# Transposes in 64 by 64 blocks, scores by v in one step, and a new order with other holds and buffers

## The chip, the cores and the metric

The kernel runs on one core of a Trainium2 chip. The metric is the device time of one execution in microseconds; lower is better. About 1% (2.1 us) is what a measurement of this kernel can tell from no change.

## What is computed

A gated linear recurrence per batch and head gives x, and x goes through a two-matrix layer with a rational activation. Batch 4, 8 heads, 768 steps, head size 48; 3072 tokens of width 384; hidden width 2048.

```
f = 1 / (1 + exp(-f_logit))
for t in range(768):
    state = f[:, :, t, :, None] * state + outer(k[:, :, t], v[:, :, t])
    y[:, :, t] = q[:, :, t] @ state
x = y, heads side by side, (3072, 384)
h = x @ w_in                                   # (3072, 2048)
P = a0 + a1*h + a2*h**2 + a3*h**3
Q = 1 + |b0|*|h| + |b1|*h**2
out = (P / (Q + 1e-6)) @ w_out                 # (3072, 384) float32
```

## The kernel before

The work is cut into 12 units: three stretches of 256 steps for each of 4 batches. Unit n belongs to batch n % 4. A unit has two halves (j = 0, 1) of 128 steps; a partition holds two neighbouring steps (i = 0, 1), so 64 partitions stand for one half.

Each unit goes through the same steps. In the order of the data:

- `ld` loads f, k, q (queue of SyncE) and v (GpSimd's queue). `ef`, `ls` (ScalarE) make log-forget-gates, `cs` (TensorE) their running sums, `A` (ScalarE) the exponentials of them.
- `xa` multiplies q or k by these into `qk`, a half of the heads or all at a time, on VectorE or, with the letter p, on GpSimd. `vm` copies a piece of v into another layout, on either.
- `T` (TensorE) transposes `qk` into PSUM, `Te` copies it to SBUF (mostly ScalarE).
- `sc` (TensorE) makes the scores of two head pairs, `mk` (VectorE) multiplies them by the mask out of PSUM into `scm`. `yb` (TensorE) adds scores by v into y, `yi` adds q by the incoming state. `ic`, `si` (TensorE) and `st` (VectorE) make the next state. `ye` copies y out as x.
- `h` (TensorE) makes 4 of 16 blocks of the hidden layer in one PSUM slot, `hy` (ScalarE) copies them to SBUF. `p1`, `p2`, `pm` (VectorE) and `sq` (VectorE) or `sa` (ScalarE) build the numerator, `ab` and the sum `zv` (VectorE) or `zd` (an adding transfer issued by GpSimd) the denominator. `rq` (ScalarE) takes its reciprocal, `tv` (VectorE) or `ta` (an adding transfer) completes the numerator, `gm` (VectorE) multiplies. `o` (TensorE) makes the output, `oe` copies it, `so` stores it.

In the profile lines these are: `T` is L347, `Te` L357 and L358, `sc` L370, `mk` L378, `yb` and `yi` L391, `ic` L436, `si` L446, `st` L461, `xa` L333, `vm` L385, `h` L477, `hy` L489, `sq` L493, `sa` L498, `ab` L502, `zv` L507, `zd` L511, `rq` L516, `p1` L526, `p2` L531, `pm` L536, `ta` L540, `tv` L544, `gm` L548, `o` L557, `oe` L567, w_out loads L221, v loads L209.

What stands in which order on each engine is written out by hand in the table `ORDER`: steps with unit, range and PSUM slot (`@`). Each engine works through its own steps strictly in that order and waits only for data and buffers. Besides, a step can be marked (`!m3`) and another held behind the mark (`^m3`): the held one begins only when the marked instruction is done. Buffers of a unit come from rings; unit n uses buffer n modulo the ring's size:

```
for key, n in (("hy", 3), ("h2", 2), ("z", 2), ("g", 3), ("qi", 2)):
    rings(key, n, [KF, NT], BF16)
```

Of the kernel before, what the change touches and what calls it, by code (L numbers as in the profile page):

```python
# [8 lines left out]
F32 = mybir.dt.float32  # L9
# [10 lines left out]
cu 1; cz 1; ld 0 f 2 4; ld 0 v; ab_ b s; cz 3; cz 0; ld 0 f 0 2; ci; ld 0 q 2 4; ld 1 f; cu 0; ld 0 k 0 2  # L20
ef 0 2 4; ls 0 2 4; cm; ld 0 k 2 4; cz 2; fa; cs 0 2 4 @0; ef 0 0 2; ls 0 0 2; ld 0 q 0 2; cs 0 0 2 @1; ld 1 k
A 0 1 0 2; A 0 1 2 4; A 0 0 2 4; A 0 0 0 2; fr; ld 2 f; ef 1; xa 0 1 2 4; ls 1; xa 0 0 2 4; vm 0 v; cs 1 @2
xa 0 0 0 2; ld 1 q; xa 0 1 0 2 !m0; ld 1 v ^m0; ld 3 f; ic 0 @3; wi 2 8 16; A 1 1; wi 3 8 16; A 1 0
T 0 0 2 @0; st 0 0; ld 2 q; ab_ a s; wi 1 8 16; xa 1 1 2 4; T 0 2 4 @1; wi 0 8 16; Te 0 0 2 s; sc 0 0 @2
xa 1 0 0 2; Te 0 2 4 s; xa 1 0 2 4; ef 2; si 0 1; sc 0 1 @0; xa 1 1 0 2; st 0 1; T 1 @1; mk 0 0; ld 2 k
mk 0 1 !m5; yb 0 0 2 @3; yi 0 1; Te 1; ef 3; yb 0 2 4; ic 1 @2; ls 2; st 1 0 !m1; sc 1 1 @0; ld 2 v ^m1
ye 0 s; cs 2 @1; mk 1 1 !m3; ls 3; sc 1 0 @3; wi 0 0 8; A 2 0; si 1 1; ld 5 f; cs 3 @0; wi 3 0 8; st 1 1
A 2 1; vm 1 v !m4; wi 2 0 8; mk 1 0; xa 2 0 0 2 p ^m0; A 3 0; h 0 8 12 @2; wi 1 0 8; xa 2 0 2 4; h 0 12 16 @1
hy 0 8 12; cz 4; fb; ld 4 f; yb 1 0 2 @3; hy 0 12 16; yb 1 2 4; xa 2 1; yi 1 1; ye 1 s; p1 0 8 16; T 2 @2
A 3 1; ab 0 8 16; h 1 12 16 @1; Te 2 s; sq 0 8 16; h 1 8 12 @3; p2 0 8 16; hy 1 12 16; pm 0 8 16 !m2; ld 3 q  # L30
ic 2 @0; hy 1 8 12; vm 2 ^m2; sc 2 1 @2; st 2 0; sc 2 0 @1; mk 2 1 !m7; ld 3 k; si 2 1; ef 5; h 0 0 4 @3
st 2 1; ls 5; ld 6 f; ab 1 8 16; h 0 4 8 @2; ef 4; tv 0 8 16; hy 0 0 4; ld 4 k; xa 3 0 2 4 p ^m3; h 1 4 8 @0
mk 2 0; ls 4; ld 4 q; ld 3 v ^m3; hy 0 4 8; h 1 0 4 @3; xa 3 1; ld 4 v; hy 1 4 8; xa 3 0 0 2; yb 2 0 2 @1
ld 7 f; zv 0 8 16; hy 1 0 4; T 3 @2; p1 0 0 8; ef 6; yi 2 1; yb 2 2 4; sq 1 0 8; Te 3 s; cs 4 @0; ld 8 f
ye 2 s; ab 1 0 8; sc 3 0 @3; cs 5 @2; A 4 0; ab 0 0 8 !m11; xa 4 0 2 4 p ^m2; mk 3 0; A 4 1; ic 3 @1
sa 1 8 16; h 2 8 12 @0; st 3 0; ld 5 k; sq 0 0 8; si 3 1; h 2 12 16 @3; hy 2 8 12; pm 0 0 8; zd 0 0 8; ld 5 q
xa 4 1 2 4 p ^m5; ls 6; sc 3 1 @0; st 3 1 !m6; A 5 1; ld 6 k; vm 3 ^m4; mk 3 1; h 2 4 8 @1; ld 5 v; hy 2 12 16
xa 4 1 0 2; ef 7; yi 3 1 @0; xa 4 0 0 2; yb 3 0 2; wo 12 16; p1 1 8 16; hy 2 4 8; T 4 @3; wo 8 12
pm 1 8 16 !m13; A 5 0; ic 4 @1; wo 4 8; xa 5 1 0 2 p ^m6; si 4 0; Te 4 s; yb 3 2 4; st 4 0; ye 3 !m10
xa 5 1 2 4 p ^m7; si 4 1; sc 4 1 @2; h 2 0 4 @3; ld 7 k; mk 4 1; vm 4 ^m3; tab 1; rq 0 0 16; wo 0 4; sc 4 0 @0  # L40
p2 0 0 8 !m12; xa 5 0 2 4 p ^m6; yb 4 2 4 @2; st 4 1; xa 5 0 0 2 p ^m6; mk 4 0; si 5 0 @1; yi 4 0; ic 5
st 5 0; yb 4 0 2; tv 0 0 8 !m8; si 5 1; hy 2 0 4; h 3 4 8 @0; ld 6 q; ld 6 v ^m8; st 5 1; gm 0 0 8; yi 4 1
h 3 8 12 @3; zd 1 0 8; tab 0; ls 7; p1 1 0 8; h 3 12 16 @1; ye 4 s; gm 0 8 16; hy 3 4 8; zv 1 8 16; T 5 @2
# [12 lines left out]
si 7 0 @0; ic 7; p1 4 8 16; yb 6 2 4 @3; ld 10 f; ab 4 8 16; o 2 0 4 8; xa 7 0 2 4; yi 6 0; zd 3 0 8; ld 8 v
pm 3 0 8; yb 6 0 2; o 2 0 0 4; tab 0; A 8 0; st 7 0; o 2 1 12 16; zd 3 8 16; ef 9; ab 4 0 8; yi 6 1; si 7 1
p2 3 0 16; A 8 1; o 2 1 4 8; o 2 1 8 12; ye 6 s; p1 4 0 8; h 5 0 4 @1; ls 9; ta 3 0 8; st 7 1; oe 2 0 2 s
vm 7 v; T 7 @3; tv 3 8 16; hy 5 0 4; cs 9 @0; Te 7 s; p1 5 8 16; h 5 4 8 @2; pm 4 8 16; A 9 1; A 9 0
xa 8 0 !m16; sc 7 0 @1; ef 10; xa 8 1 2 4 p ^m16; sc 7 1 @3; h 6 12 16 @0; mk 7 0; ld 11 q; hy 5 4 8; ld 11 f  # L60
zd 4 0 8; p2 4 0 8 !m19; so 2 0 2; ls 10; h 6 4 8 @1; xa 9 0 0 2 p ^m19; mk 7 1; hy 6 12 16; h 6 8 12 @2
pm 4 0 8; yi 7 1 @0; yb 7 0 2; sq 5 8 16; tab 1; rq 3 0 8; ta 4 0 8; yi 7 0; yb 7 2 4; xa 9 0 2 4; h 6 0 4 @3
xa 8 1 0 2; ye 7 s; p1 5 0 8; hy 6 8 12; ab 5 0 8; h 7 4 8 @0; gm 3 0 8; hy 6 0 4; h 7 0 4 @2; hy 6 4 8
p2 4 8 16; zv 4 8 16; rq 3 8 16; T 8 @3; ta 4 8 16; ld 10 q; ld 10 v; o 3 1 0 4 @1; sq 5 0 8; ld 10 k; ld 9 v
o 3 1 4 8; hy 7 0 4; gm 3 8 16; o 3 0 0 4; Te 8 s; o 3 0 4 8; zd 5 0 8; p2 5 0 8; si 8 0 @2; hy 7 4 8
o 3 1 12 16; sq 6 0 8; o 3 1 8 12; rq 4 0 16; sc 8 1 @3; ab 5 8 16 !m18; xa 9 1 0 2 p ^m18; sc 8 0 @0
o 3 0 12 16; mk 8 1; xa 9 1 2 4 p ^m16; o 3 0 8 12; mk 8 0 !m21; ic 8; vm 8 ^m17; cs 10 @3; st 8 0; zd 5 8 16
# [561 lines left out]
```

## Time and profile before

| | |
|---|---|
| median of 3 runs | 212.77 us (212.0 to 214.08) |
| the profiled execution | 213.87 us, span of the profile 212.2 us |
| granted TensorE clock | 0.994 |
| TensorE (PE) busy | 190.1 us, 90% |
| VectorE (DVE) busy | 190.8 us, 90% |
| ScalarE (ACT) busy | 186.7 us, 88% |
| GpSimd (POOL) busy | 81.5 us, 38% |
| transfers | 43.15 MB, mean 203 GB/s |

Busy time is the union of an engine's instructions over the span. TensorE's matmuls overlap one another, so the time that a group of them takes is read from the start of its first to the start of what follows. The time of an execution is somewhat longer than the span of its instructions, here by 1.7 us.

### The profile page before, as it was taken

The page shows a single profiled execution, that of the slowest core. Times are in us where ns is not written, and L with a number is a line of the kernel's source. Part 1 is how long each engine was busy: PE and PEld are TensorE (multiplying, and loading weights), DVE is VectorE, ACT ScalarE, POOL GpSimd, SP SyncE. Part 2 cuts the span into 40 slices and gives each one's busy share as a digit, 9 for nine tenths or more (in the row PEclk, how much of TensorE's full clock was granted, in tenths as well). Part 3 has the DMA queues.
Part 4 walks back from the last instruction along what each step waited for, and adds up shares of the span by engine and source line. Part 5 has one row for each costly group of instructions (what it writes and reads, how often), then busy time and mean ns, then how long its engine had stood idle before and what let it go on. Part 6 is the DMA issues. An engine that isn't in the chain of part 4 may idle for free.

```text
span 212.2 us, 6607 instructions
## 1 busy us (share of the span) xinstructions
PE 190.1 (90%) x2894; PEld 138.7 (65%) x2894; DVE 190.8 (90%) x236; ACT 186.7 (88%) x172; POOL 81.5 (38%) x99
## 2 busy tenths in 40 slices
PE   1296799997789999999999899999999999999991
PEld 1165587875568678766888567678766766775650
DVE  3269689999999999999999979999999999999970
ACT  4755689999887999999999699999999999999861
POOL 6050612329943438016351750551583433402000
PEclk9999999999999999999999999999999999999997
DMA  5999998999999189999999999799899999998955
GB/s 93 276 251 208 249 223 229 246 259 199 180 204 209 37 153 153 228 283 279 206 232 253 245 199 219 163 195 205 171 195 162 211 206 195 198 197 167 235 152 170
DMA packets 61820, 43.15 MB, mean 203 GB/s; under 512 B 51424, under 2 KB 56544, under 8 KB 61792
## 3 DMA queue, kind: packets, MB, share of 16 engines
q0 software_dynamic: 20528, 23.86, 68.4%
q1 hardware_dynamic: 41184, 18.78, 34.2%
q8 instruction: 22, 0.36, 0.6%
q10 hardware_dynamic: 80, 0.10, 0.2%
q14 instruction: 6, 0.05, 0.1%
HBM read 25.17 MB, written 4.72 MB: 141 GB/s over the span
## 4 chain that ended last, share of the span: by engine, by line
PE 60%; DVE 15%; DMA 12%; ACT 5%; issue 3%; POOL 3%; SPq 2%; POOLq 0%; ACTq 0%; DVEq 0%
PE op L557 28%; PE hp L477 19%; DMA w_in_sb<-in_moe_w_in_dram 5%; PE y L391 4%; DMA g<-hy 4%; DVE scm L378 3%; DMA k<-in_k_dram 3%; PE tp L347 3%; DVE qkp L333 2%; DVE g L536 2%; PE sc L370 2%; PE cs L306 2%; DVE h L493 2%; ACT qi L516 2%; DVE state L461 1%
## 5 line engine op out<-in xcount | busy, mean ns | idle before, releaser
L477 PE MATMUL hp<-x,w_in_sb 128*128 128x256 bf16 x576 | 68.0, 273 | 1.1 <-DVE state L461 0.9
L557 PE MATMUL op<-w_out_sb,g 128*128 128x384 bf16 x384 | 68.6, 326 | 0.0
L477 PEld LDWEIGHTS <-w_in_sb 128*128 128x128 bf16 x576 | 55.5, 98 | 10.4 <-issue 1.9
L489 ACT CAST hy<-hp 128x1024 bf16<-128x1024 f32 x48 | 47.8, 1027 | 5.0 <-PE hp L477 3.1
L557 PEld LDWEIGHTS <-g 128*128 128x128 bf16 x384 | 35.8, 98 | 23.8 <-issue 1.2
L516 ACT ACTIVATE qi<-z 128x4096 bf16<-128x4096 bf16 (+1 forms) x16 | 44.4, 2777 | 1.1 <-DVE z L507 1.1
L511 POOL DMA_DIRECT2D z<-h x20 | 21.5, 1120 | 26.1 <-ACT h L498 18.1
L378 DVE TENSOR_TENSOR scm<-sc,mask 128x1024 bf16<-128x1024 f32 x24 | 28.8, 1214 | 1.5 <-PE sc L370 1.4
L548 DVE TENSOR_TENSOR g<-g,qi 128x2048 bf16<-128x2048 bf16 (+2 forms) x24 | 28.9, 1217 | 0.9 <-ACT qi L516 0.7
L536 DVE TENSOR_TENSOR g<-g,h 128x2048 bf16<-128x2048 bf16 (+1 forms) x21 | 29.4, 1401 | 0.1
L498 ACT ACTIVATE h<-hy 128x2048 bf16<-128x2048 bf16 (+1 forms) x13 | 26.8, 2072 | 0.0
L540 POOL DMA_DIRECT2D g<-hy x15 | 13.8, 938 | 28.1 <-DVE g L536 10.4
L328 ACT ACTIVATE A<-cs 128x768 f32<-128x768 f32 (+3 forms) x26 | 19.0, 779 | 4.5 <-PE cs L314 4.5
L333 POOL TENSOR_TENSOR qkp<-k,A 128x384 bf16<-128x384 f32 x11 | 13.0, 1218 | 23.4 <-DVE g L548 10.6
L306 PE MATMUL cs<-lsp,Ui 128*128 128x384 bf16 (+1 forms) x39 | 11.1, 345 | 10.4 <-ACT lsp L296 10.4
L526 DVE TENSOR_SCALAR g<-hy,a_sb 128x2048 bf16<-128x2048 bf16 (+1 forms) x23 | 19.0, 832 | 0.6 <-ACT hy L489 0.6
L209 POOL DMA_DIRECT2D v<-in_v_dram x12 | 12.4, 1037 | 17.6 <-DVE state L461 8.8
L531 DVE TENSOR_SCALAR hy<-hy,a_sb 128x2048 bf16<-128x2048 bf16 (+1 forms) x20 | 18.6, 928 | 0.4
L333 POOL TENSOR_TENSOR qkp<-q,A 128x384 bf16<-128x384 f32 x10 | 12.6, 1268 | 9.9 <-ACT A L328 5.3
L502 DVE TENSOR_SCALAR z<-hy 128x2048 uint16<-128x2048 uint16 (+1 forms) x21 | 15.7, 759 | 0.0
L347 PE MATMUL tp<-ident,qkp 128*128 128x128 bf16 x192 | 13.7, 227 | 2.0 <-DVE qkp L333 1.4
L391 PE MATMUL y<-scm,v 64*32 64x128 bf16 x384 | 14.0, 218 | 0.8 <-DVE scm L378 0.7
(71 smaller groups left out, 245.0 us busy)
## 6 DMA issues: line engine op xcount, KB each, us to landing
z<-h POOLq DMA_DIRECT2D x20, 512.0 KB, 7.2
g<-hy POOLq DMA_DIRECT2D x15, 512.0 KB, 7.5
f<-in_f_logit_dram SPq DMA_DIRECT2D x11, 384.0 KB, 6.9
k<-in_k_dram SPq DMA_DIRECT2D x11, 384.0 KB, 8.2
q<-in_q_dram SPq DMA_DIRECT2D x11, 384.0 KB, 7.5
v<-in_v_dram POOLq DMA_DIRECT2D x12, 192.0 KB, 7.3
out_dram<-f SPq DMA_DIRECT2D x12, 192.0 KB, 3.6
out_dram<-osb SPq DMA_DIRECT2D x10, 192.0 KB, 5.0
```

Of the source, the lines that this page charges most:

```text
L333: i = (nc.gpsimd if eng == "p" else nc.vector).tensor_mul(s["qk"][:, x, :, hh, 0:D], s["qk"[x]][:, hh].rearrange("p h i d -> p i h d"), s[ ...
L347: nc.tensor.transpose(t[:, x, i, p, :], s["qk"][:, x, i, 2 * p:2 * p + 2, :].rearrange("t h d -> t (h d)"), ident)
L378: return nc.vector.tensor_mul(t, s["sc", g].rearrange("s r a i t -> s (r a) (i t)"), mb)
L391: nc.tensor.matmul(s["y"][32 * a:32 * a + 32, j, kk * C:kk * C + C].rearrange("e (i t) -> e i t", i=2), lhsT, rhs, start=(j, a) not in s[" ...
L477: nc.tensor.matmul(t[:, m - m0, :].rearrange("f (j t) -> f j t", j=UB), w_in_sb[:, kk, m * P:(m + 1) * P], s["x"][:, :, kk, :], start=(kk ...
L489: nc.scalar.copy(fl(big(s, "hy"), m0, m1), fl(s["hp", m0], 0, m1 - m0))
L498: return nc.scalar.activation(fl(big(s, "h2"), m0, m1), fl(big(s, "hy"), m0, m1), AF.Square)
L511: return nc.gpsimd.dma_start(out=fl(big(s, "z"), m0, m1), in_=fl(big(s, "h2"), m0, m1), accum_op=ALU.add)
L516: return nc.scalar.add_instruction(mybir.InstActivation(name=nc.get_next_instruction_name(), func=AF.Reciprocal, ins=[nc.scalar.lower_ap(f ...
L536: return nc.vector.tensor_mul(fl(big(s, "g"), m0, m1), fl(big(s, "g"), m0, m1), fl(big(s, "h2"), m0, m1))
L548: return nc.vector.tensor_mul(fl(big(s, "g"), m0, m1), fl(big(s, "g"), m0, m1), fl(big(s, "qi"), m0, m1))
L557: nc.tensor.matmul(s["op", g][:, j, 0:DM], big(s, "g")[:, m, C * j:C * j + C], w_out_sb[:, m, :], start=(s["on", j] == 1), stop=(s["on", j ...
```

## The change

Five things are edited.

1. `T` transposes blocks of 64 rows (one half's steps) by 64 columns (one head, padded from 48) instead of 128 by 128: 64 transpositions per unit instead of 16. PSUM and SBUF tiles get the half j as their first index, so that the two row halves write different PSUM banks. `sc` and `yi` read the new layout.
2. `yb` of a unit is one step over all four head pairs instead of two steps over two.
3. The ring `hy` has four buffers instead of three, `z` three instead of two. The ring `qi` is gone: `rq` writes its reciprocal over z, and `gm` reads z.
4. The marks and holds of GpSimd's products are others.
5. The whole `ORDER` is written anew. The steps and their division among the engines stay, with these exceptions: three more pairs of `p1`, two of `ab` and three of `gm` are one instruction each, `ye 0` goes from ScalarE to VectorE, the first half of the last `oe` too. The unused `dm` and the memset of `zz` go.

```diff
-for key, n in (("hy", 3), ("h2", 2), ("z", 2), ("g", 3), ("qi", 2)):
+for key, n in (("hy", 4), ("h2", 2), ("z", 3), ("g", 3)):
     rings(key, n, [KF, NT], BF16)
-rings("T", 1, [2, 2, HP, P], BF16)
+rings("T", 1, [UB, 2, 2, HP, R], BF16)
...
 def T(n, *args):
-    t = s["tp", a0] = slot(sl, [P, 2, 2, HP, P], BF16, "tp")
+    t = s["tp", a0] = slot(sl, [P, UB, 2, 2, HP, R], BF16, "tp")
     for x in (1, 0):
         for i in range(2):
             for p in range(a0, a1):
-                nc.tensor.transpose(t[:, x, i, p, :],
-                                    s["qk"][:, x, i, 2 * p:2 * p + 2, :].rearrange("t h d -> t (h d)"), ident)
+                for j in range(UB):
+                    m = slice(R * j, R * j + R)
+                    for par in range(2):
+                        nc.tensor.transpose(t[E * par:E * par + E, j, x, i, p, :],
+                                            s["qk"][m, x, i, 2 * p + par, :], ident[m, m])
...
 def sc(n, g, sl):
-    s["T"][r, 1, i0, 2 * g + a, m], s["T"][r, 0, :, 2 * g + a, m],
+    s["T"][r, j, 1, i0, 2 * g + a, :], s["T"][r, j, 0, :, 2 * g + a, :],
...
 def yi(n, j, sl=None):
-    ymm(s, j, a, kk, state(s, j)[:, a, 32 * kk:32 * kk + 32], s["T"][:, 0, :, a, R * j:R * j + R])
+    ymm(s, j, a, kk, state(s, j)[:, a, 32 * kk:32 * kk + 32], s["T"][:, j, 0, :, a, :])
...
 def rq(n, m0, m1):
-    outs=[nc.scalar.lower_ap(fl(big(s, "qi"), m0, m1))]
+    outs=[nc.scalar.lower_ap(fl(big(s, "z"), m0, m1))]
...
 def gm(n, m0, m1):
-    return nc.vector.tensor_mul(fl(big(s, "g"), m0, m1), fl(big(s, "g"), m0, m1), fl(big(s, "qi"), m0, m1))
+    return nc.vector.tensor_mul(fl(big(s, "g"), m0, m1), fl(big(s, "g"), m0, m1), fl(big(s, "z"), m0, m1))
...
 ORDER (some steps of it)
-xa 3 0 2 4 p ^m3      (m3 is mk 1 1)
+xa 3 0 2 4 p ^m3      (m3 is pm 0 8 16)
-yb 5 0 2; yb 5 2 4
+yb 5 0 4
```

Two places of the new order. The first is on VectorE in the middle of the early part, where the hidden layer of unit 0 goes on beside `xa` of unit 4 (`qkp0` and `qkp1` are the two `qk` buffers, `h2` the squares, `scm` the masked scores). Before:

```order
L378 TENSOR_TENSOR scm0_133<-sc_944,mask_76 128x1024
L461 TENSOR_TENSOR state3_1_96<-sv_981,A1_131 128x384
L493 TENSOR_TENSOR h20_109<-hy0_106 128x2048
L536 TENSOR_TENSOR g0_113<-g0_113,h20_109 128x2048
L461 TENSOR_TENSOR state3_2_97<-sv_981,A1_131 128x384
L378 TENSOR_TENSOR scm0_133<-sc_1035,mask_76 128x1024
L333 TENSOR_TENSOR qkp0_80<-k1_122,A0_130 128x2x4x48
L333 TENSOR_TENSOR qkp0_80<-q1_125,A0_130 128x2x4x48
L526 TENSOR_SCALAR g1_114<-hy1_107,a_sb_98 128x2048
L536 TENSOR_TENSOR g1_114<-g1_114,h21_110 128x2048
```

and with the change:

```order
L378 TENSOR_TENSOR scm0_132<-sc_1149,mask_76 128x1024
L329 TENSOR_TENSOR qkp0_79<-q1_124,A0_129 128x2x4x48
L487 TENSOR_TENSOR h20_109<-hy0_105 128x2048
L461 TENSOR_TENSOR state3_1_95<-sv_1167,A1_130 128x384
L530 TENSOR_TENSOR g0_114<-g0_114,h20_109 128x2048
L461 TENSOR_TENSOR state3_2_96<-sv_1167,A1_130 128x384
L378 TENSOR_TENSOR scm0_132<-sc_1227,mask_76 128x1024
L329 TENSOR_TENSOR qkp0_79<-k1_121,A0_129 128x2x4x48
L520 TENSOR_SCALAR g1_115<-hy1_106,a_sb_97 128x2048
L530 TENSOR_TENSOR g1_115<-g1_115,h21_110 128x2048
```

The product with q (`xa 4 0 0 2`) has moved from behind the product with k to a place five instructions earlier, right behind the first mask product; the rest is nearly as it was.

The second is on ScalarE where unit 7's hidden layer begins (`hy`), around the copy of T of unit 8. Before:

```order
L516 ACTIVATE qi1_117<-z1_112 128x2048
L489 CAST hy1_107<-hp_2354 128x1024
L357 COPY T0_132<-tp_2371 128x1024
L489 CAST hy1_107<-hp_2339 128x1024
L516 ACTIVATE qi0_116<-z0_111 128x4096
```

and with the change:

```order
L510 ACTIVATE z0_111<-z0_111 128x2048
L357 COPY T0_131<-tp_2754 128x1024
L483 CAST hy3_108<-hp_2735 128x1024
L483 CAST hy3_108<-hp_2719 128x1024
L510 ACTIVATE z1_112<-z1_112 128x4096
```

The copy of T now stands ahead of both `hy`, and unit 7 writes the fourth `hy` buffer instead of the second, which the transfer `ta 4 8 16` reads.

More of the change, by code (lines that the diff above doesn't have):

```diff
@@ L95 @@
[L95 to L98 removed]
+ci; cz 0; ld 0 f 0 2; cu 1; ld 0 f 2 4; cz 3; cz 2; ab_ b s; cz 1; ld 0 v; ld 1 f; ld 0 k 0 2; cu 0
@@ L99 @@
+gm 11 0 4; o 11 1 8 12; gm 11 4 8; so 10 0 2; o 11 0 0 4; o 11 0 4 8; o 11 1 0 4; oe 11 0 1 v; o 11 1 4 8
+so 11 0 1; oe 11 1 2 s; so 11 1 2
 """
@@ L152 @@
     hsel = consts.tile([P, UB, 2, 2], BF16, name="hsel")
-    zz = consts.tile([P, 512], BF16, name="zz")
     qkp = [consts.tile([P, 2, 2, H, E], BF16, name=f"qkp{i}") for i in range(2)]
@@ L253, in const_z @@
                 nc.vector.memset(ind[R * j:R * j + R, j, :], 1.0)
-        elif i == 4:
-            return nc.vector.memset(zz, 0.0)
         else:
@@ L354, in Te @@
         s["T"] = ring["T"][n % len(ring["T"])]
-        dst, src = (t[:, :, :, a0:a1].rearrange("p x i a t -> p (x i) (a t)") for t in (s["T"], s["tp", a0]))
+        dst, src = (t[:, :, :, :, a0:a1].rearrange("p j x i a t -> p (j x i) (a t)") for t in (s["T"], s["tp", a0]))
         if "s" in args:
@@ L464, in st @@
             _at(s["ae"], [[DM + 16 if n else DM // 2 + 8, 2], [1, 4], [0, D]], 4 * j))
-    def dm(i, sl):
-        t = slot(sl, [P, 2, 512], F32, "dm")
-        for b in range(2):
-            nc.tensor.matmul(t[:, b, :], zz[:, 0:P], zz, start=True, stop=True)
     def h(n, m0, m1, sl):
@@ L521, in rq @@
                  mybir.ImmediateValue(dtype=F32, value=0.0)],
-            outs=[nc.scalar.lower_ap(fl(big(s, "qi"), m0, m1))]))
+            outs=[nc.scalar.lower_ap(fl(big(s, "z"), m0, m1))]))
     def p1(n, m0, m1):
```

156 lines of the change are left out of this document (76 added, 80 removed).

## The prediction

> **What bounds the kernel now.** I read the page first, then busy time by stage, then the chain that ended last, and from there the places where that chain loses time.
>
> ```profile
> PE 190.1 (90%) x2894; PEld 138.7 (65%) x2894; DVE 190.8 (90%) x236; ACT 186.7 (88%) x172; POOL 81.5 (38%) x99
> ```
>
> Three engines are full to 88 or 90%, so no single one explains the span. The stages tell them apart (columns: length, then busy time and instructions of PE, PEld, DVE, ACT and POOL, granted clock, DMA share, GB/s):
>
> ```profile
> 29.30:61.00 31.70, 27.74 (x561) 21.73 (x557) 31.52 (x34) 29.53 (x31) 17.22 (x18) 1.00 1.16 222
> 61.00:107.00 46.00, 45.90 (x689) 33.65 (x689) 45.88 (x54) 44.07 (x41) 16.92 (x17) 1.00 1.01 195
> 107.00:130.00 23.00, 21.59 (x397) 16.48 (x386) 21.45 (x23) 21.30 (x20) 10.82 (x12) 1.00 1.17 230
> 130.00:190.00 60.00, 60.00 (x799) 43.18 (x797) 59.25 (x62) 59.10 (x46) 24.20 (x26) 1.00 1.01 193
> ```
>
> From 29.3 to 61 us VectorE is full (31.52 of 31.70) and TensorE is not (27.74). After 61 us both are full, but for one dent between 107 and 130. The chain says the same (start, length, who):
>
> ```profile
> 29.30 0.81 DVE g L526
> ...
> 61.15 0.63 PE y L391 x32
> ...
> 66.44 0.89 PE tp L347 x16
> ...
> 111.76 8.62 DMA g<-hy
> ...
> 189.58 18.24 PE op L557 x112
> ```
>
> It runs on VectorE up to 61 us, then on TensorE, leaves it once for a transfer (8.62 us) and ends in a row of 112 output products. So a saving on VectorE counts in full before 61 us; after 61 us only what both engines save counts.
>
> **Term 1: VectorE beside GpSimd's products, before 61 us.** The timeline of both engines there, and the same operations later, when GpSimd was doing something else:
>
> ```profile
> 36.00 1.35 POOL L333 TENSOR_TENSOR qkp<-q,A 128x384 bf16<-128x384 f32 x1 [1.64 <-ACT lsp L296]
> 36.41 2.02 DVE L544 TENSOR_TENSOR g<-g,hy 128x2048 bf16<-128x2048 bf16 x1
> 38.35 1.21 DVE L378 TENSOR_TENSOR scm<-sc,mask 128x1024 bf16<-128x1024 f32 x1
> ...
> 50.60 1.38 DVE L333 TENSOR_TENSOR qkp<-k,A 128x384 bf16<-128x384 f32 x1
> 51.16 2.38 POOL L221 DMA_DIRECT2D w_out_sb<-in_moe_w_out_dram  x3
> 51.91 1.35 DVE L333 TENSOR_TENSOR qkp<-q,A 128x384 bf16<-128x384 f32 x1
> ...
> 53.42 3.42 POOL L333 TENSOR_TENSOR qkp<-k,A 128x384 bf16<-128x384 f32 x2
> 54.16 1.83 DVE L536 TENSOR_TENSOR g<-g,h 128x2048 bf16<-128x2048 bf16 x1
> ...
> 103.15 1.22 DVE L544 TENSOR_TENSOR g<-g,hy 128x2048 bf16<-128x2048 bf16 x1
> 105.01 1.22 DVE L536 TENSOR_TENSOR g<-g,h 128x2048 bf16<-128x2048 bf16 x1
> 112.53 0.54 DVE L333 TENSOR_TENSOR qkp<-q,A 128x384 bf16<-128x384 f32 x1
> ```
>
> `tv` costs 2.02 - 1.22 = 0.80 us too much, `pm` 1.83 - 1.22 = 0.61, the two `xa` 1.38 - 0.54 = 0.84 and 1.35 - 0.54 = 0.81: together 3.06 us, all in the stage that VectorE sets. The first two lie under GpSimd products, the last two under the issuing of the v and w_out loads. GpSimd pays as well: 3.42 us for two products. The mask product `scm` reads PSUM and takes 1.21 us wherever it stands.
>
> The change holds each of these products behind the VectorE instruction ahead of a mask or state product. `xa 3 0 2 4 p` now starts behind `pm 0 8 16`, and `st 2 0`, `mk 2 1`, `mk 2 0` follow on VectorE before anything sensitive. `xa 5 1 2 4 p` comes to GpSimd only after three w_out issues (2.38 us), while VectorE passes `xa 4 1 0 2`, `p1` and `pm 1`; `xa 5 1 0 2 p` is held behind `pm 1`. So the 0.80 and the 0.61 should go. One of the two `xa` moves to an earlier place, behind `mk 3 0`, where GpSimd issues a v load alone; I count its 0.81 as gone and the other's 0.84 as left, since the w_out issues still stand beside it. That is 2.2 us, of bounds 0 (the holds miss, or the waiting moves) and 3.1. Behind a held product GpSimd's queue keeps its later work: v loads, w_out, `zd` and `ta` transfers; the transposes of that unit wait for the product itself. TensorE has 31.70 - 27.74 = 4.0 us of slack here to cover that, ScalarE 2.2.
>
> **Term 2: fewer VectorE instructions.** Three more pairs of `p1` become one instruction each:
>
> ```profile
> L526 DVE TENSOR_SCALAR g<-hy,a_sb 128x2048 bf16<-128x2048 bf16 x22 | 17.6, 808 | 0.6 <-ACT hy L489 0.6
> L526 DVE TENSOR_SCALAR g<-hy,a_sb 128x4096 bf16<-128x4096 bf16 x1 | 1.3, 1343 | 0.0
> ```
>
> 2 x 808 - 1343 = 273 ns each, 0.8 us for three; neighbours overlap a little (36.41 + 2.02 is past 38.35), so 0.6. The like merging of `ab` and `gm` I leave at nothing. The extra `ye 0` on VectorE falls before 29.3 us, where VectorE is not full; the `zz` memset that goes lies there too. The first output half of the last unit moves from ScalarE to VectorE after VectorE's last product. All three count nothing; without that cover `ye` would cost about 1 us (its bounds: 0 and a mask product, 1.21).
>
> **Term 3: the dent at 107 to 130.** From the list of waits (total, times, longest) and the timeline:
>
> ```profile
> ACT hy L489 <- DMA g<-hy: 1.6, 1, 1.6
> DVE scm L378 <- PE sc L370: 1.4, 2, 0.9
> DVE g L548 <- ACT qi L516: 0.7, 2, 0.5
> ...
> 121.54 0.32 PE L446 MATMUL sv<-state,ident 128*128 128x384 bf16 x1 [0.93 <-ACT hy L489]
> ```
>
> With three `hy` buffers unit 7 writes the one that unit 4's `ta` transfer still reads (8.62 us, in the chain). ScalarE stands 1.6 us, behind it queue the copy of T and the next `hy`, TensorE stands 0.93 and VectorE up to 0.9. With four buffers unit 7 writes one that unit 3 used, and T's copy is now issued ahead of that `hy`. VectorE idles 1.4 + 0.7 = 2.1 us in the waits listed; I take 1.0 for this one, bounds 0 (another wait in its place) and 2.1. `qi` goes; its place is taken by z, with three buffers, which VectorE itself frees before it writes again.
>
> **Term 4: TensorE after 61 us.** Rows of its timeline; the difference of two starts is what a group really takes:
>
> ```profile
> 66.27 1.06 PE L347 MATMUL tp<-ident,qkp 128*128 128x128 bf16 x16
> 67.17 0.33 PE L306 MATMUL cs<-lsp,Ui 128*128 128x384 bf16 x1
> ...
> 79.65 0.24 PE L391 MATMUL y<-scm,v 64*32 64x128 bf16 x4
> 80.48 0.30 PE L436 MATMUL sv<-v,qkp 64*128 64x96 bf16 x6
> ...
> 96.91 0.24 PE L391 MATMUL y<-scm,v 64*32 64x128 bf16 x4
> 97.47 0.82 PE L557 MATMUL op<-w_out_sb,g 128*128 128x384 bf16 x4
> ...
> 100.92 1.46 PE L557 MATMUL op<-w_out_sb,g 128*128 128x384 bf16 x8
> 102.22 1.47 PE L477 MATMUL hp<-x,w_in_sb 128*128 128x256 bf16 x12
> ...
> 106.73 0.64 PE L370 MATMUL sc<-T 48*64 48x128 bf16 x32
> 107.30 4.10 PE L477 MATMUL hp<-x,w_in_sb 128*128 128x256 bf16 x36
> ...
> 121.70 1.46 PE L557 MATMUL op<-w_out_sb,g 128*128 128x384 bf16 x8
> 123.10 0.70 PE L370 MATMUL sc<-T 48*64 48x128 bf16 x32
> ```
>
> Eight output products take 1.30 us ahead of other full-array work (100.92 to 102.22) and 1.40 ahead of tiled work (121.70 to 123.10): entering a tiled shape costs 0.10. Transposes cost 0.90 per unit now (66.27 to 67.17) and enter nothing. Sixty-four blocks of 64x64 were never run here. The nearest row is `sc`, of the same tile shape and twice as wide: 32 in 0.57, leaving included, 17.9 ns each. Upper bound 64 x 17.9 = 1.15; lower, half of that for half the width, 0.57; with the 0.10, 0.67 to 1.25. I take the middle, 0.96: 0.06 more per unit, 0.4 us for the seven units transposed after 61 us.
>
> The scores by v: 32 of a half take 0.56 (96.91 to 97.47), 0.66 with entering; two halves next to each other 0.83 (79.65 to 80.48), 0.93 with entering. Merged, all eight tiles of the array can work at once: 0.56 to 0.83, with entering 0.66 to 0.93. Of the units after 61 us five had their halves apart (6, 7, 9, 10, 11: 1.32 each) and two together (5 and 8: 0.93). Saved: 5 x 0.39 to 0.66 and 2 x 0 to 0.27, so 2.0 to 3.8 us; I take 2.6. TensorE is thus relieved by 2.6 - 0.4 = 2.2 us, more than the 1.6 of terms 2 and 3, so VectorE's 1.6 is what counts after 61 us.
>
> The Trainium skill ("TensorE: Matmul & The Clock Gate", on LDWEIGHTS and on fast weight load) prices a weight load at its columns over 1.2 in ns and grants the fast load only to 128 columns. By it a 64-column load would be an estimated 53 ns, and four tiles at once would give some 13 ns per transposition, near the upper bound above; `sc`, whose loads are as wide, cannot tell, since its products hide such a load.
>
> **Sum.** 2.2 + 0.6 + 1.0 = 3.8 us. The profiled execution took 213.87 us (span 212.2, 1.7 around it), 1.1 over the median of 212.77; taken from the median, 209.0 us.
>
> **Rivals.**
> 1. All of it comes: 3.1 of contention, 0.6, all 2.1 of the waits: 5.8 us, **207.0**. For it: TensorE and ScalarE have slack before 61 us. Against: the w_out issues stay beside an `xa`.
> 2. The blocks go at `sc`'s pace: 7 x 0.35 = 2.5 us more, which eats the 2.6 saved. TensorE then gives nothing after 61 us, the 1.6 of terms 2 and 3 turns into VectorE waiting, and only 2.2 is left: **210.6**. For it: same tiles, same weight width. Against: the moving side is half as wide. [...]
> 3. The tight holds make GpSimd late: a product that misses its mask product waits for the next VectorE gap, at least one `scm`, 1.21 us, and T with it. Two such waits on TensorE, 2.4 us, leave 1.4 of the gain: **211.4**; the change then doesn't do what it says. For it: GpSimd's queue is one line. Against: it is idle most of the time (81.5 us busy).
> 4. Slower: transposing blocks do not run side by side. Each then takes half of today's 0.90/16 = 56 ns, 28 ns, and 64 of them 1.8 us, 1.9 with entering: 1.0 more per unit, 7.0 us, less 2.6 for the scores by v. TensorE is 4.4 us longer after 61 us, terms 2 and 3 are lost, term 1 gives 2.2 back: **215.0**. It decides from (0.90 + 2.6/7 - 0.10)/64 = 18 ns per block on, where TensorE's relief is gone. For it: no row shows a transposition in tiles. Against: `sc` does run four at a time.
>
> **Numbers.** Chances: forecast 0.40, rival 1 0.15, rival 2 0.18, rival 3 0.14, rival 4 0.13. A measurement of this kernel tells about 1% from no change, 2.1 us: the line is 210.6 below and 214.9 above. Faster: 0.36 of the forecast's, all of rival 1, half of rival 2: 0.60. Slower: rival 4 and 0.02 of rival 3: 0.15. The rest, 0.25, is within 1%. The range runs from below rival 1 to short of rival 4: 206.0 to 214.0.
>
> **What would show it.** Right: a transposing group of 0.7 to 1.25 us from start to next start; scores by v at most 0.83 for 64; `tv` and `pm` at 1.22 before 61 us; no wait of `hy` for `g<-hy`; VectorE still the fullest engine up to some 59 us. Wrong: a transposing group near 1.9 us, new waits of TensorE for `qkp` from GpSimd, or VectorE instructions of 1.3 us and more that lie under GpSimd work in new places.

## The result and the profile after

The changed kernel took 221.06 us (median of 4 runs, 218.83 to 221.37), the kernel before 213.43 on the same chip (4 runs). The ratio is 1.0358, with a 95% interval of 1.0252 to 1.0465: 3.6% slower. The forecast was 209.0 us in a range of 206.0 to 214.0, so both the direction and the range were wrong. The profiled execution took 221.36 us, span 219.7. Medians here and below are over all executions; the ratios with their intervals leave out executions in a slower state of the chip, and it is the ratios that count.

Engine totals of the page first, to be held against the first quoted line of the prediction:

```profile
PE 188.8 (86%) x3470; PEld 134.4 (61%) x3470; DVE 189.6 (86%) x229; ACT 185.2 (84%) x170; POOL 77.5 (35%) x99
```

Every engine has less to do than before (TensorE 188.8 us for 190.1, VectorE 189.6 for 190.8, ScalarE 185.2 for 186.7), and yet the span is 7.5 us longer. Nothing was added to an engine's busy time; what grew is the time in which none of them is full. The same windows as in the prediction (the first starts at 27.10; columns as there):

```profile
27.10:61.00 33.90, 28.88 (x732) 22.93 (x734) 29.44 (x38) 29.45 (x33) 13.62 (x18) 0.95 1.02 192
61.00:107.00 46.00, 43.40 (x796) 30.44 (x792) 44.26 (x49) 43.45 (x38) 18.78 (x20) 1.00 1.07 204
107.00:130.00 23.00, 22.09 (x442) 16.21 (x440) 22.44 (x27) 22.50 (x21) 10.18 (x13) 1.00 1.15 208
130.00:190.00 60.00, 55.45 (x986) 38.26 (x984) 54.92 (x51) 54.30 (x44) 21.11 (x25) 0.97 1.01 189
```

Before, TensorE was busy for all 60.00 us of the last window; now for 55.45, and VectorE and ScalarE lose as much (54.92, 54.30). When three engines that feed each other all fall behind at once, it is worth asking whether one of them stands still for a reason of its own. The chain that ended last gives a candidate (its summary by engine, before and then after; and of the chain after, start, length and who of its two largest pieces with no releaser):

```profile
PE 60%; DVE 15%; DMA 12%; ACT 5%; issue 3%; POOL 3%; SPq 2%; POOLq 0%; ACTq 0%; DVEq 0%
```

```profile
PE 58%; DVE 19%; DMA 10%; issue 8%; ACT 2%; POOL 1%; POOLq 0%; DVEq 0%; ACTq 0%
...
30.89 2.39 issue
...
150.00 2.48 issue
```

"issue" is time in which the engine waited for nothing that the profile shows. It was 3% of the chain before and is 8% now. Less than half of the 8%, 7.9 us of 17.8, is TensorE's, in the pauses that follow, so the share alone proves little: it is still 6.8% in the version of experiment 1 below, which is as fast as the kernel before. The timeline of TensorE at the second of these places:

```profile
146.13 2.79 PE L471 MATMUL hp<-x,w_in_sb 128*128 128x256 bf16 x24
148.85 0.71 PE L347 MATMUL tp<-ident,qkp 64*64 64x64 bf16 x64
149.50 0.50 PE L471 MATMUL hp<-x,w_in_sb 128*128 128x256 bf16 x3
152.48 0.82 PE L471 MATMUL hp<-x,w_in_sb 128*128 128x256 bf16 x3 [2.48 <-issue]
```

TensorE does the 64 blocks of one unit in 149.50 - 148.85 = 0.65 us, three of the `hp` products behind them, and then stands 2.48 us in the middle of a row of equal products: same weights tile, same moving tile, same output, no semaphore. The list of TensorE's waits (total, times, longest) has seven such pauses of over 0.3 us under "issue":

```profile
PE hp L471 <- issue: 3.4, 2, 2.5
PE y L391 <- issue: 3.1, 3, 1.3
PE tp L347 <- issue: 2.4, 1, 2.4
PE op L551 <- issue: 0.4, 1, 0.4
```

That is 9.25 us together (1.30, 2.39, 0.92, 0.38, 0.82, 2.49 and 0.95), 5.56 us of them after 61 us. The list of before has none.

Where they stand tells what they are. TensorE's matmuls counted from one pause to the next (length, busy time and count, clock, DMA share, GB/s):

```profile
19.20:33.20 14.00, 9.58 (x255) 0.99 1.19 217
33.20:69.10 35.90, 31.58 (x767) 0.96 1.05 195
69.10:75.70 6.60, 6.19 (x127) 1.00 1.33 202
75.70:132.50 56.80, 54.55 (x1024) 1.00 1.07 205
132.50:152.40 19.90, 17.44 (x384) 1.00 1.02 216
152.40:169.40 17.00, 15.98 (x255) 0.90 0.95 157
```

255, 767, 127, 1024, 384, 255: multiples of 128 within one. The odd ones come from 17 semaphore and drain instructions that stand in the same stream: with every weight load, matmul and such instruction of TensorE counted, all seven pauses stand at place 193 or 194 of a block of 256. The page's DMA queues, before and then after, show a queue that brings instructions:

```profile
q8 instruction: 22, 0.36, 0.6%
```

```profile
q8 instruction: 27, 0.44, 0.8%
```

0.44 MB in 27 packets is 16 KB each. The change adds 3470 - 2894 = 576 matmuls with as many weight loads, 1152 instructions, and five packets: about 230 instructions a packet, which fits the 256 of the count, 64 bytes each, or 128 pairs of load and matmul. So the pauses stand where one block of instructions ends and the next begins. The records of all DMA queues around the pause at 150 us, first while TensorE works through the last block that it has, then while it stands (kind: packets, MB, share):

```profile
q0 software_dynamic: 225, 0.79, 92.6%
...
```

```profile
q1 hardware_dynamic: 185, 0.26, 91.1%
q8 instruction: 1, 0.02, 5.4%
...
```

From 145.7, where TensorE enters the block, to 150.2 no instruction packet moves, while GpSimd's queue fills 92.6% of the DMA engines' time; the packet comes between 150.2 and 151.3, when TensorE is already dry, and 1.3 us after its landing TensorE goes on. Over the trace of after, each block's packet starts between 0.9 us before and 4.6 us after TensorE enters the block ahead of it, and takes about 0.95 us; behind each of the seven pauses the next block begins 1.2 to 1.7 us after the landing, and nowhere earlier than that. Together that is up to some 7 us, while a block lasts 6.5 us in the median now (8.0 before). Before, its 128 pairs were mostly long, and TensorE reached the end later than the packet; now 64 pairs pass in 0.65 us. One block of the kernel before, too, begins 1.3 us after its packet's landing with 1.24 us of idle ahead of it, at 22.7 us; the profile puts that idle to ScalarE, so it is not in the count above.

### The profile page after: what moved, and what is told of

It reads as the page before. It is cut to its first block, busy times and chain, and to the rows that moved or that the text cites. A ratio compares the mean times of both kernels' runs of the same rounds, so it can differ in the third digit from the quotient of the medians.

```text
span 219.7 us, 7754 instructions
## 1 busy us (share of the span) xinstructions
PE 188.8 (86%) x3470; PEld 134.4 (61%) x3470; DVE 189.6 (86%) x229; ACT 185.2 (84%) x170; POOL 77.5 (35%) x99
## 4 chain that ended last, share of the span: by engine, by line
PE 58%; DVE 19%; DMA 10%; issue 8%; ACT 2%; POOL 1%; POOLq 0%; DVEq 0%; ACTq 0%
PE op L551 21%; PE hp L471 21%; DMA v<-in_v_dram 10%; PE y L391 5%; DVE g L530 3%; PE cs L302 3%; PE sc L370 3%; DVE g L542 3%; PE tp L347 3%; DVE g L538 2%; DVE g L520 2%; PE sv L436 2%; DVE h L487 2%; DVE hy L525 2%; DVE z L496 2%
## 5 line engine op out<-in xcount | busy, mean ns | idle before, releaser
L471 PE MATMUL hp<-x,w_in_sb 128*128 128x256 bf16 x576 | 70.5, 279 | 6.1 <-issue 3.4
L471 PEld LDWEIGHTS <-w_in_sb 128*128 128x128 bf16 x576 | 56.4, 100 | 16.5 <-issue 6.6
L510 ACT ACTIVATE z<-z 128x4096 bf16<-128x4096 bf16 (+1 forms) x16 | 44.7, 2791 | 0.1
L505 POOL DMA_DIRECT2D z<-h x20 | 19.5, 1025 | 29.7 <-ACT h L492 14.2
L542 DVE TENSOR_TENSOR g<-g,z 128x2048 bf16<-128x2048 bf16 (+2 forms) x21 | 28.5, 1370 | 0.8 <-ACT z L510 0.5
L329 POOL TENSOR_TENSOR qkp<-k,A 128x384 bf16<-128x384 f32 x11 | 11.0, 1025 | 25.5 <-DVE z L496 10.8
L520 DVE TENSOR_SCALAR g<-hy,a_sb 128x2048 bf16<-128x2048 bf16 (+1 forms) x20 | 18.4, 922 | 1.4 <-ACT hy L483 1.1
L302 PE MATMUL cs<-lsp,Ui 128*128 128x384 bf16 (+1 forms) x39 | 11.8, 363 | 8.3 <-ACT lsp L292 8.3
L461 DVE TENSOR_TENSOR state<-sv,A 128x384 bf16<-128x384 f32 x20 | 11.0, 550 | 6.0 <-PE sv L436 5.1
L357 ACT COPY T<-tp 128x1024 f32<-128x1024 f32 (+1 forms) x12 | 11.4, 962 | 4.3 <-PE tp L347 4.3
```

What stands on the lines that cost most here:

```text
L329: i = (nc.gpsimd if eng == "p" else nc.vector).tensor_mul(s["qk"][:, x, :, hh, 0:D], s["qk"[x]][:, hh].rearrange("p h i d -> p i h d"), s[ ...
L471: nc.tensor.matmul(t[:, m - m0, :].rearrange("f (j t) -> f j t", j=UB), w_in_sb[:, kk, m * P:(m + 1) * P], s["x"][:, :, kk, :], start=(kk ...
L510: return nc.scalar.add_instruction(mybir.InstActivation(name=nc.get_next_instruction_name(), func=AF.Reciprocal, ins=[nc.scalar.lower_ap(f ...
L520: return nc.vector.tensor_scalar(fl(big(s, "g"), m0, m1), fl(big(s, "hy"), m0, m1), a_sb[:, 3:4], a_sb[:, 2:3], op0=ALU.mult, op1=ALU.add)
L542: return nc.vector.tensor_mul(fl(big(s, "g"), m0, m1), fl(big(s, "g"), m0, m1), fl(big(s, "z"), m0, m1))
```

## The experiments

The main theory (F, where a text gives it a letter) is this one, **supply**: TensorE runs out of instructions at the ends of blocks, because 64 short pairs per unit use a block up too fast. The rivals are those of the prediction, and that the new order and holds make the start and GpSimd's queue late (O in the texts), above all a **late start**: the new table puts `vm 0` on VectorE ahead of the first gate products, where it waits for v's load, and the first `hp` product stands at 26.9 us instead of 25.4. Ratios are to the kernel before on the same chip. Pauses are those of over 0.3 us that the list of waits puts to "issue".

**1. The change with its transposes back at 128x128** (16 per unit, old layout of T; everything else as in the change).

```diff
-                    for j in range(UB):
-                        m = slice(R * j, R * j + R)
-                        for par in range(2):
-                            nc.tensor.transpose(t[E * par:E * par + E, j, x, i, p, :],
-                                                s["qk"][m, x, i, 2 * p + par, :], ident[m, m])
+                    nc.tensor.transpose(t[:, x, i, p, :],
+                                        s["qk"][:, x, i, 2 * p:2 * p + 2, :].rearrange("t h d -> t (h d)"), ident)
...
```

> The change with its transposes put back to 16 of 128 by 128 per unit (layout of T, sc and yi as before too); its order, holds, buffers and merged yb stay. Theory F (TensorE runs out of instructions: they come in blocks of 16 KB, and a group of 64 tiled pairs at 8 ns each uses one up faster than the next arrives): 576 pairs fewer, so the seven pauses of TensorE over 0.3 us that wait for no semaphore (9 us in sum in the change's trace) go or shrink to under 2 us, and the time falls by 4 to 7 us, to 214 to 217, although each transposing group itself is 0.25 us longer. Theory O (the new order and holds make the start and GpSimd's queue late): nothing of that is touched, the groups are longer by 7 x 0.25 us, so 221 to 223.

Measured: 213.38 us (10 runs), ratio 1.0009 [0.996, 1.0057]; 22 instruction packets. Two pauses are left:

```profile
PE sc L366 <- issue: 2.0, 1, 2.0
PE hp L467 <- issue: 0.8, 1, 0.8
```

Their 2.83 us are more than the under 2 us expected, and the time fell by more than expected. The larger one stands at 23 us, at the block end where the kernel before idles 1.24 us. The 3.5% between 1.0358 and 1.0009, 7.4 us, come with the 64x64 blocks. That the rest of the change then ends at no gain instead of 0.98 is a second finding, taken up below.

**2. The kernel before with only its transposes in 64x64 blocks** (the reverse edit, with T, Te, sc and yi in the new layout).

> The kernel before with only its transposes in 64 by 64 blocks (and the layout that goes with it); order, holds, buffers and halved yb as before. Theory F: pauses of TensorE without a semaphore appear, at least three of them over 0.5 us, and the time rises by 2 to 6 us, to 215 to 219. Theory O: the transposing groups are 0.25 us shorter and nothing else changes: 211 to 213.

Measured: 218.44 us (4 runs), ratio 1.0228 [1.0129, 1.0327]. Four pauses, 5.39 us. Matmuls between them, and the last pause on the timeline:

```profile
18.79:32.20 13.41, 10.93 (x255) 0.80 1.20 237
32.20:61.10 28.90, 25.43 (x639) 1.00 1.04 199
61.10:166.20 105.10, 100.92 (x1919) 1.00 1.04 199
```

```profile
164.08 0.22 PE L395 MATMUL y<-scm,v 64*32 64x128 bf16 x3
166.21 0.27 PE L395 MATMUL y<-scm,v 64*32 64x128 bf16 x5 [1.91 <-issue]
```

255, 639, 1919 are 2, 5 and 15 times 128, less one. This pause cuts one group of eight products of scores by v into three and five: neither the tiles read nor the tile written change there. So the blocks, with the layout that goes with them, cost 2.3% in the old order too, with none of the change's other parts: this slowdown isn't an affair of the new table.

**3. The change with 64 tiny products at the idle start**, which move every later instruction half a block along (the new step's entry in the list of steps is left out here).

```diff
+    def pad(i, sl):
+        t = slot(sl, [P, 2, 512], F32, "pad")
+        for x in range(i):
+            nc.tensor.matmul(t[:, 0, 0:4], ident, ident[:, 0:4], start=True, stop=True)
...
-ld 0 q 2 4; ef 0 0 2; ld 0 k 2 4; ef 0 2 4; ls 0 0 2; ls 0 2 4; cs 0 2 4 @0; ld 0 q 0 2; cs 0 0 2 @1
+ld 0 q 2 4; ef 0 0 2; ld 0 k 2 4; ef 0 2 4; ls 0 0 2; ls 0 2 4; pad 64 @3; cs 0 2 4 @0; ld 0 q 0 2; cs 0 0 2 @1
```

> The change with 64 tiny products (4 columns) more on TensorE at its idle start, 1.6 us of work there; they only shift every later instruction by half a 16 KB block. The output is not touched. Theory F: the pauses without a semaphore stand at other groups than in the change (by number of the product: some of the seven vanish, others come), their sum 4 to 12 us, and the time moves by over 1 us either way. Theory O: the same waits at the same groups, time plus at most 1 us.

Measured: 222.23 us (4 runs), ratio 1.0431 [1.0314, 1.0547]. Five pauses, 8.66 us. Between the last four:

```profile
36.00:47.10 11.10, 10.27 (x255) 1.00 0.76 158
47.10:59.60 12.50, 9.20 (x256) 1.00 1.11 198
59.60:138.10 78.50, 71.30 (x1407) 0.98 1.06 198
```

2, 2 and 11 times 128 within one. The pauses stay on the grid of 128 and so left every step of the program at which they had stood: they belong to the count of instructions, not to an operation, a tile or a wait that the profile fails to show. Which block ends come late changes with the shift. The time does not improve; whether it got worse by the 1 us expected cannot be told, since the interval overlaps that of the change.

**4. The change with blocks of 64 rows by 128 columns**: 32 pairs per unit, not 64.

```diff
-                        for par in range(2):
-                            nc.tensor.transpose(t[E * par:E * par + E, j, x, i, p, :],
-                                                s["qk"][m, x, i, 2 * p + par, :], ident[m, m])
+                        nc.tensor.transpose(t[:, j, x, i, p, :],
+                                            s["qk"][m, x, i, 2 * p:2 * p + 2, :].rearrange("t h d -> t (h d)"),
+                                            ident[m, m])
```

> The change with blocks of 64 rows by 128 columns (both heads of a pair at once, still one half of the steps): 32 transposing pairs per unit instead of 64, 384 pairs fewer in all. Theory F (TensorE runs out of instructions at the ends of 16 KB blocks, 128 pairs each): two blocks run side by side, so a group still takes about 0.6 us, but a group uses up only a quarter of a block; the pauses without a semaphore fall from 9 us to under 4, and the time to 214 to 217. Rival (64-row blocks cost TensorE time in themselves, by switching shapes): the pauses and the time stay as in the change, 219 to 222.

Measured: 214.52 us (10 runs), ratio 1.0004 [0.9949, 1.0059]. Three pauses are left, 3.46 us, and 24 packets. By time it cannot be told from the 128x128 transposes; by pauses it stands between them and the 64x64 blocks (2.83, 3.46, 9.25 us). It keeps the change's layout of T, `Te`, `sc` and `yi`, so that layout is not what costs the time. Its 32 blocks take 0.57 us per unit, less than the 0.65 of the 64. It starts its first `hp` at 25.0 us where the 128x128 version did at 27.2, which may hide part of what its pauses cost.

**5 and 6. The late start.** First the change with `vm 0` put behind the first four gate products; then the version of experiment 1 with the whole order of before up to the first transposes. The diff is that of the first.

```diff
-A 0 0 2 4; A 0 1 2 4; ld 1 k; vm 0 v; ef 1; fa; A 0 1 0 2; ls 1; ld 1 q; cm; A 0 0 0 2; cs 1 @2; fr
-xa 0 1 2 4; xa 0 1 0 2; xa 0 0 2 4; ld 2 f; xa 0 0 0 2 !m0; ld 1 v ^m0; ic 0 @3; A 1 1; A 1 0; T 0 0 2 @0
+A 0 0 2 4; A 0 1 2 4; ld 1 k; ef 1; fa; A 0 1 0 2; ls 1; ld 1 q; cm; A 0 0 0 2; cs 1 @2; fr
+xa 0 1 2 4; xa 0 1 0 2; xa 0 0 2 4; ld 2 f; xa 0 0 0 2 !m0; ld 1 v ^m0; vm 0 v; ic 0 @3; A 1 1; A 1 0; T 0 0 2 @0
```

> The change with one step moved: the copy vm 0, which waits for the load of v, goes from ahead of the four xa of unit 0 on VectorE to behind them. Both theories take the start for 1.7 us of the loss (first hidden-layer product at 27.1 us instead of 25.4). Theory O: that gain arrives at the end, 219 to 220. Theory F: it arrives only as far as the pauses of TensorE fall as before; each may move, so 217 to 222.

> The change with 128 by 128 transposes and, besides, the steps of the old order up to the first transposition (loads, constants, first xa; the copy vm 0 behind the first xa). With 128 by 128 transposes alone it took 213.4 us, first hidden-layer product at 27.2 us instead of 25.4, the clock at 0.54 to 0.61 from 22 to 30 us. If the late start is what ate the gain of the other edits, the first hidden-layer product comes at about 25.5 us and the time is 211 to 212. If the other edits bring nothing, 212.5 to 214.

Measured: 220.18 us (4 runs), ratio 1.0362 [1.0256, 1.0468] for the first, whose first `hp` comes at 26.5 us and whose six pauses still add up to 8.28. For the second 213.28 us (12 runs), 0.9973 [0.9934, 1.0011], first `hp` at 25.4. Putting the old start back is worth about 0.4% (1.0009 to 0.9973), and the intervals overlap; the late start does not explain the slowdown.

**7 to 11. The other parts alone, in the kernel before.** Scores by v merged (each unit's `yb n 0 2` and `yb n 2 4` become one `yb n 0 4` in the place of the second); four `hy` buffers and three of z in place of `qi`; seven GpSimd products held behind the VectorE step just ahead of them; and two pairs of these. Of the buffers the line with the rings is shown, of the holds one of the seven. They are not the change's own marks: in the old order `xa 3 0 2 4` is held behind `tv`, in the change behind `pm 0 8 16`, and two of the seven have a mark there that lies far back.

```diff
-    for key, n in (("hy", 3), ("h2", 2), ("z", 2), ("g", 3), ("qi", 2)):
+    for key, n in (("hy", 4), ("h2", 2), ("z", 3), ("g", 3)):
```

```diff
-st 2 1; ls 5; ld 6 f; ab 1 8 16; h 0 4 8 @2; ef 4; tv 0 8 16; hy 0 0 4; ld 4 k; xa 3 0 2 4 p ^m3; h 1 4 8 @0
+st 2 1; ls 5; ld 6 f; ab 1 8 16; h 0 4 8 @2; ef 4; tv 0 8 16 !m24; hy 0 0 4; ld 4 k; xa 3 0 2 4 p ^m24; h 1 4 8 @0
```

> The kernel before with one edit: scores by v of all four head pairs in one step, at the place of the later of its two steps. My prediction: TensorE relieved by 2.0 to 3.8 us after 61 us, of which VectorE lets 0 to 1 through: 211.5 to 213. Rival (dense groups of 64 tiled pairs run out of instructions, as the 64 by 64 transposes do): one to three pauses without a semaphore, 213 to 216.

> The kernel before with the rings alone: hy four, z three, the reciprocal written over z; its own order. My prediction took 1.0 us (0 to 2.1) for the wait of hy for the transfer that reads its buffer: 211.8 here. Rival: the wait turns into another one, 212.5 to 213.5.

> The kernel before with seven of GpSimd's products (units 3, 4 and 5, 36 to 66 us) held behind the VectorE instruction just ahead of them, as the change does; nothing else differs, and no instruction is added on TensorE. Term 1 of the prediction says: tv at 36.4 us falls from 2.02 to 1.22 us, pm at 54.2 from 1.83 to 1.22, one of the two xa stays long; 1.4 to 2.2 us less, ratio 0.990 to 0.993. Rival, tight holds make GpSimd late: the transposes of units 3 to 5 wait for its products, ratio 1.000 to 1.006, with a new wait of TensorE for qkp. Supply of instructions: no pause of TensorE without a semaphore in either case.

> The kernel before with four hy buffers and three z (measured alone at 0.992) and the seven holds. If the holds act in another stage than the buffers, the gains add: 0.982 to 0.985. If what the holds win before 61 us is taken back by the wait that comes next, 0.990 to 0.994, the same as the buffers alone. No pause of TensorE without a semaphore.

> The kernel before with four hy buffers and three z, and the scores by v of all pairs of heads in one step. Alone the merged step measured 1.0025 and the buffers 0.992. If TensorE's relief of 2 us or more after 61 us needs the dent at 107 to 130 us gone to reach the end, 0.978 to 0.985. If merging costs elsewhere what it saves (all scores wait for the second mask product), 0.992 to 0.997.

| in the kernel before | median us (runs) | ratio [95%] |
|---|---|---|
| scores by v merged | 215.05 (12) | 1.0025 [0.9981, 1.0069] |
| four `hy`, three z | 212.14 (12) | 0.9917 [0.988, 0.9954] |
| seven holds | 211.97 (6) | 0.989 [0.9837, 0.9942] |
| buffers and holds | 211.00 (12) | 0.9817 [0.9773, 0.9861] |
| buffers and merged scores | 213.18 (12) | 0.994 [0.9903, 0.9978] |

Against what was expected of the versions with holds, these too have pauses: one of 0.32 us with the holds, 2.26 with buffers and holds; further one of 1.81 with the buffers and 1.97 with buffers and merged scores. All stand at a block's end before 28 us. Merged scores alone have none, so the rival there, that they run out of instructions, is not borne out. The buffers close the dent at 107 to 130 us, where TensorE had 21.59 busy us of 23.00:

```profile
107.00:130.00 23.00, 23.00 (x421) 17.93 (x410) 22.89 (x25) 22.94 (x22) 10.82 (x12) 1.00 1.18 229
```

The holds free VectorE in the stage that it sets. Its timeline there, for `tv`, two `xa` and `pm`:

```profile
35.34 1.22 DVE L544 TENSOR_TENSOR g<-g,hy 128x2048 bf16<-128x2048 bf16 x1
...
49.44 0.55 DVE L333 TENSOR_TENSOR qkp<-k,A 128x384 bf16<-128x384 f32 x1
49.90 0.55 DVE L333 TENSOR_TENSOR qkp<-q,A 128x384 bf16<-128x384 f32 x1
51.28 1.23 DVE L536 TENSOR_TENSOR g<-g,h 128x2048 bf16<-128x2048 bf16 x1
```

2.02, 1.38, 1.35 and 1.83 us had stood there: all four are back at their price. The two parts add, 1.8% together, and that version beats both kernels of this study. Merging the scores by v brings nothing, alone or with the buffers; the 211.5 to 213 us expected of it alone were not reached. The rows of the merged kernel without the buffers suggest why:

```profile
61.00:107.00 46.00, 45.44 (x719) 32.97 (x720) 45.86 (x54) 43.84 (x41) 16.47 (x18) 1.00 0.97 184
...
130.00:190.00 60.00, 59.25 (x855) 42.93 (x841) 59.58 (x61) 59.97 (x48) 24.54 (x26) 1.00 1.05 202
```

TensorE now has slack there (45.44 of 46.00, 59.25 of 60.00), and VectorE (45.86 and 59.58) and, in the last window, ScalarE (59.97) are as full as before, so they do not let the relief through. That the scores now all wait for the second mask product was the other reading; no run separates the two.

## Why the prediction was wrong, point by point

**Term 1, VectorE beside GpSimd's products: right.** Forecast 2.2 us of bounds 0 to 3.1; seven holds alone measured 0.989, some 2.4 us, and freed all four instructions. In the change itself `tv` fell to 1.22 and one `pm` stayed long:

```profile
43.96 1.22 DVE L538 TENSOR_TENSOR g<-g,hy 128x2048 bf16<-128x2048 bf16 x1
...
54.97 0.55 DVE L329 TENSOR_TENSOR qkp<-k,A 128x384 bf16<-128x384 f32 x1
56.51 1.83 DVE L530 TENSOR_TENSOR g<-g,h 128x2048 bf16<-128x2048 bf16 x1
```

The `xa` that I had left beside the w_out issues is free, and `pm` stands beside them instead (1.83 - 1.22 = 0.61 us left, not 0.84): the wrong one of the two, nearly the same sum. That such issues slow what stands beside them is no rule, though: with the seven holds `pm` (1.23 us from 51.28) lies under the same three issues, 50.37 to 52.96 us, and runs at its price.

**Term 2, merged p1 pairs: the price as worked out, not tried alone.** Four of the wide form now take 1339 ns each:

```profile
L520 DVE TENSOR_SCALAR g<-hy,a_sb 128x4096 bf16<-128x4096 bf16 x4 | 5.4, 1339 | 0.3 <-PE op L551 0.3
```

**Term 3, four `hy` buffers: right, and nearer its upper bound.** Forecast 1.0 of 0 to 2.1; alone 0.9917, some 1.8 us. In the change no `hy` waits for `g<-hy` any more.

**Term 4, TensorE after 61 us: its durations were right, its account was not.** Sixty-four blocks take 0.65 us with leaving, 0.75 with the 0.10 of entering: inside the 0.67 to 1.25, under the 0.96 taken. So rival 2 (`sc`'s pace) and rival 4 (blocks not side by side, 1.9 us) are both false. From the price of a weight load in the Trainium skill ("TensorE: Matmul & The Clock Gate", on LDWEIGHTS) the prediction worked out an estimated 13 ns per transposition; the trace does not agree, it has 0.65 / 64 = 10.2 ns, leaving included. (13 ns also lies in the middle of the bounds, 64 x 13 = 0.83 us between 0.57 and 1.15, and not near the upper one.) The scores by v, 64 in one step:

```profile
102.68 0.25 PE L391 MATMUL y<-scm,v 64*32 64x128 bf16 x8
...
103.13 0.28 PE L391 MATMUL y<-scm,v 64*32 64x128 bf16 x8
103.34 0.35 PE L391 MATMUL y<-T,state 128*32 128x128 bf16 x12
```

103.34 - 102.68 = 0.66 us, inside 0.56 to 0.83. **The step that failed is the one that followed:** "TensorE is thus relieved by 2.6 - 0.4 = 2.2 us". It priced an instruction by the time that it streams and took 1152 more instructions to be free of charge otherwise. They cost 4.9 us in the kernel before (1.0228) and 7.4 us in the change (1.0358 against 1.0009), in pauses that no term and no rival had. Rival 4 had the right sign by the wrong mechanism: it is luck that one of the rivals pointed the way that the time went. The relief itself was not needed: the buffers gain without it, and without the pauses it brought nothing.

**What hung on a pause.** The one at 150 us delays the `hp` that ScalarE reads, and with it the scores whose masks VectorE waits for (total, times, longest; both longest ones follow this pause):

```profile
ACT hy L483 <- PE hp L471: 7.7, 7, 3.9
DVE scm L378 <- PE sc L370: 4.6, 4, 3.6
```

Nor does TensorE go on at full speed. Windows ahead of this pause and behind it (length, busy time and count, granted clock, DMA share, GB/s):

```profile
146.00:150.00 4.00, 4.00 (x115) 1.00 0.97 185
152.40:154.00 1.60, 1.52 (x8) 0.50 1.07 207
154.00:156.00 2.00, 2.00 (x12) 0.56 0.75 141
156.00:158.00 2.00, 2.00 (x20) 1.00 1.06 199
```

The granted clock is 0.50 and 0.56 for 3.6 us and then 1.00 again: 1.60 x 0.50 + 2.00 x 0.44 = 1.7 us of full speed lost on top of the 2.48. So one pause becomes 3.9 us of ScalarE's waiting and 3.6 of VectorE's.

**Rival 3, tight holds that make GpSimd late: small, but there.** A v load queued behind a held product comes late, and the state products wait for it, in the change and with the seven holds alone:

```profile
PE sv L436 <- DMA v<-in_v_dram: 2.8, 2, 2.0
```

```profile
PE sv L436 <- DMA v<-in_v_dram: 0.8, 1, 0.8
```

The longer of the change's two waits (2.0) ends at 22.4 us and belongs to the late start; the other, 0.8, at 62 us. The kernel before has none. So the holds bring one such wait in the old order too, and it is small beside what they win there (0.989).

**What stays open.** Terms 1 to 3 were forecast at 3.8 us; buffers and holds alone measure 1.8%, 3.9 us. Yet the change without its 64x64 blocks is even with before. Some 4 us are lost in the rest of the new table, whose moves the prediction counted at nothing. One profiled execution of each shows roughly where: the 97th `hp` product starts at 47.6 us in experiment 1 and at 45.1 before, the 145th at 62.2 and 62.0, the 337th at 116.3 and 114.3, the 385th at 139.2 and 139.6. So VectorE's stage and the dent win over 2 us each, as terms 1 and 3 say, and 2.5 us are lost ahead of 47 us and 1.8 between 62 and 116. Seen ahead of 47 us are waits of the state products for `qkp` (1.3 us) and for the late v load (0.9 us), a pause of 2.02 us and the clock at 0.50 from 22 to 29 us; the old start put back in experiment 6 was still worth only about 0.4%. Later there is a pause of 0.81 us and a wait of `hp` for `x` of 0.9. I did not try these one by one, so their shares are not shown. Open too is why an instruction packet starts at once in one block and 5 us late in another; at 150 us GpSimd's queue filled the DMA engines meanwhile. Over the 261 blocks that TensorE enters after 29 us in all traces here, that queue took 0.51 of the DMA engines' time in the first us where the packet started within 1 us, 0.96 where it started after 3 to 4, but 0.74 where it came later still: a tie, not a proof, and no run varied it.

## What to carry to other kernels

An instruction costs its place in the stream as well as its time on the engine: before an edit that cuts one operation into many short ones, count the added instructions, divide by the block that the instruction queue's packets show, and ask how long TensorE takes for a block at its densest place. Look for pauses that wait for no semaphore, above all inside a row of equal instructions, and count the instructions between two of them. And try the parts of a mixed change alone: here two of them won 1.8%, and a third, which measured faster on its engine, cost 3.5%.

## What the runs showed of the hardware that was not expected

- TensorE's instructions arrived in 16 KB packets of 256, here 128 pairs of weight load and matmul. A packet took about 0.95 us, started up to 4.6 us after TensorE had entered the block ahead of it (5.4 over all traces here), and TensorE went on 1.2 to 1.7 us after its landing at the earliest. The pauses of 0.3 to 2.5 us that the profile puts to "issue" all stood at these ends.
- Transpositions in 64x64 blocks do run side by side: 10.2 ns each, leaving included, so four of them, 41 ns, do the work of one of 128x128, which takes 56 ns (0.90 us for 16). Two of 64 rows by 128 columns do it in 36 ns (0.57 us for 32).
- Behind both pauses of 2.4 to 2.5 us of the change the granted clock was 0.50 for some 3.4 us; behind the one of 0.82 us at 132 us it stayed at 1.00. It is no rule: a pause of 2.28 us at 30 us in experiment 2 and one of 2.36 us at 34 us in experiment 3 had 1.00 for 5 us behind them. TensorE can pay for a long pause a second time, and need not.
